# One tiled stretch for all K=64 tails of four row tiles, with a second xy tile in PSUM and the spectral pieces in the z banks

**Chip, cores, metric.** One core of one Trainium2 chip. Metric: device time of one execution in microseconds (us), lower is better.

## The reference

Forward and gradients of a gated sum of two branches over x (2048 x 576): a spectral filter (2-D real FFT, multiplication by a 2048 x 289 complex weight, inverse FFT) and a gated FFN of width 4608. Cut to what matters:

```python
def _A_ref(x, w_r, w_i):                      # spectral branch
    X = rfft2(x) * (w_r + 1j * w_i)
    return irfft2(X, s=(S, D))                # S, D = 2048, 576
def _B_ref(x, w_gate, w_up, w_down):          # FFN branch, F = 4608
    return (gelu(x @ w_gate) * (x @ w_up)) @ w_down
def _fwd(...):
    g = sigmoid((x * gate_w).sum(-1, keepdims=True))
    return g * _A_ref(...) + (1 - g) * _B_ref(...)
out, vjp = jax.vjp(_fwd, ...);  return out, *vjp(grad_out)
```

## The kernel before

A head transposes x and the output gradient and does the forward spectral pieces of x. Then come eighteen groups of 256 columns of F. In each group eight steps treat two row tiles (of 128 rows) each: `z` (output gradient times w_down), `xy` (x times w_gate and w_up), elementwise work on ScalarE and VectorE, and between them weight-gradient units (`wps`) of the group before and "pieces" of the spectral branch (`pf`). The last part (`acc`) reads the stored products back and is not touched. The contraction over 576 is 4 x 128 + 64; the 64-row tails of two row tiles sit in the two halves of the array (row tiling; the profile's form `64*128`). A run of such matmuls between full ones is called a tiled stretch here.

Some terms. Two steps, four row tiles, are a *pair*; a group has four. Groups are numbered from 0 and pairs from 1 through the kernel, so that pairs 1, 5, ... are the *first pairs* of groups. A piece is *evacuated* when ScalarE or VectorE has read it out of PSUM; only then can its banks be written again. The waits name a piece by what it is evacuated to: `Y` and `Vt` (forward pieces), `Xx`, `Xg` and `Vt` (middle ones), `ZT` (the first half of an inverse piece, `z(i)` in the code), `ev` and then `yo` (its second half, `d(i)`, called a d piece below). `z` in the profile is the FFN's tile alone.

The parts that matter, cut (`...`):

```python
ph = ...tile_pool(name="ph", bufs=1, space=PSUM)   # xy: 2 banks
pz = ...tile_pool(name="pz", bufs=1, space=PSUM)   # z: 2 banks
pw = ...tile_pool(name="pw", bufs=2, space=PSUM)   # weight gradients: 2 x 1 bank
pf = ...tile_pool(name="pf", bufs=1, space=PSUM)   # spectral pieces: 2 banks

def H_mm(g, tp):
    if tp % 2 == 0:
        zt[0] = pz.tile(...)
        ...  # 16 full matmuls (K=128), then the 4 tails (K=64, two at a time)
    xy = ph.tile([P, 2, 2 * FG], F32, tag="xy", name="xy")
    for tt, r in enumerate((LO, HI)):                     # row-tiled tails
        nc.tensor.matmul(xy[:, tt, :], lhsT=xT[r, 4, t0 + tt, :], rhs=wgu[r, 4, :], start=True, stop=False)
    ...  # 8 full matmuls

def d(i):   # inverse spectral piece: 4 full matmuls, 2 row-tiled
    def f():
        yps = pftile()
        ...
        nc.scalar.activation(ev[:], yps[:, 0, :DF], ACT.Copy, scale=scale)
        V.scalar_tensor_tensor(yo[:, 0:DF], yps[:, 1, :DF], scale, ev[:], op0=ALU.mult, op1=ALU.add)
        V.scalar_tensor_tensor(yo[:, D - 1:DF - 1:-1], yps[:, 1, 1:DF - 1], -scale, ev[:, 1:DF - 1], ...)
        LD.dma_start(dv[:, i, :], yo[:])
```

## Time and profile before

| | before |
|---|---|
| time, median of 3 (range) | 1528.66 us (1527.97 to 1532.15) |
| TensorE busy | 1462.9 us, 96% |
| first z matmul / first acc matmul | 61.4 / 1085.2 us |
| a group with middle spectral pieces / inverse ones / none | 54 / 56.6 to 58.6 / 48.8 us |

The group lengths are distances between the first z matmuls of groups in the trace. The lines are in the prediction. TensorE sets the time; what it loses must be sought in distances between the starts of its matmuls, as the ends are modelled. This is the stage of the inverse spectral pieces, from the windows view (window, its length, then busy us and instructions of TensorE, weight loads, VectorE, ScalarE, GpSimd, then TensorE's clock, share of the DMA engines, GB/s):

```profile
613.30:1009.10 395.80, 385.66 (x3086) 262.32 (x3136) 273.45 (x755) 249.76 (x501) 0.00 (x0) 1.00 0.44 121
```

TensorE is idle for 10 of 396 us there, at full clock.

### The profile page before, as it was taken

Reading aid. Unit: us, or ns where it says so; the run is one execution under the profiler, and the core shown is the slowest. Engines: PE = TensorE matmul, PEld = TensorE weight load, DVE = VectorE, ACT = ScalarE, POOL = GpSimd, SP = SyncE. Lnnn points to the kernel's source line nnn. Section 1 sums busy time; section 2 is a strip of 40 time slices with the busy share of each in tenths; the row PEclk is TensorE's granted clock in tenths of the full one; section 3 lists DMA queues with packets and bytes.
Section 4 is the critical chain, followed back from the end, with each engine's and each line's share of the span. In section 5 each row is a group of like instructions: output and inputs, shape, how many; then the busy total and the mean of one; then the engine's idle time right before and its main releaser. Section 6 shows DMA issues by size and latency. Waiting matters only on the chain.

```text
span 1530.2 us, 30042 instructions
## 1 busy us (share of the span) xinstructions
PE 1462.9 (96%) x11700; PEld 1052.8 (69%) x11824; DVE 845.8 (55%) x2237; ACT 699.4 (46%) x1361; POOL 21.8 (1%) x51
## 2 busy tenths in 40 slices
PE   7879998999999999999999999999998999999998
PEld 5535666666766766666666666677876777777776
DVE  6576666888888877666676666775023221211101
ACT  5565665676766766666666666664000000000000
POOL 1000000000000000000000000000000000000000
PEclk9899999999999999999999999999999999999999
DMA  5143234445445434434434434556999987878773
GB/s 182 43 113 102 84 109 125 119 132 147 135 141 146 129 115 138 119 100 120 126 99 135 135 107 123 147 131 136 265 212 213 189 164 155 173 154 170 150 154 65
DMA packets 503399, 210.49 MB, mean 138 GB/s; under 512 B 307606, under 2 KB 497112, under 8 KB 503256
## 3 DMA queue, kind: packets, MB, share of 16 engines
q1 hardware_dynamic: 499816, 202.83, 54.6%
q0 software_dynamic: 1632, 4.72, 1.2%
q8 instruction: 92, 1.51, 0.4%
q10 hardware_dynamic: 1808, 1.02, 0.2%
q14 instruction: 51, 0.42, 0.1%
HBM read 40.89 MB, written 93.82 MB: 88 GB/s over the span
## 4 chain that ended last, share of the span: by engine, by line
PE 66%; issue 24%; ACT 4%; DVE 3%; POOL 1%; SPq 1%; DMA 1%; POOLq 0%; DVEq 0%; ACTq 0%
PE wps L409 16%; PE xy L326 15%; PE z L315 8%; PE wps L392 8%; PE acc L851 3%; PE xy L323 2%; PE wps L420 2%; PE acc L893 2%; PE z L319 1%; PE pf L629 1%; PE fx L449 1%; PE pf L449 1%; PE pf L645 1%; ACT q L338 1%; ACT xb L339 1%
## 5 line engine op out<-in xcount | busy, mean ns | idle before, releaser
L326 PE MATMUL xy<-wgu,xT 128*128 128x512 bf16 x1028 | 256.1, 380 | 13.8 <-issue 10.8
L893 PEld LDWEIGHTS <-pin 128*128 128x128 bf16 x2304 | 225.4, 98 | 56.8
L409 PEld LDWEIGHTS <-xn 128*128 128x128 bf16 x2304 | 224.2, 98 | 36.7 <-issue 0.2
L326 PEld LDWEIGHTS <-xT 128*128 128x128 bf16 x1152 | 101.1, 98 | 142.7 <-issue 41.1
L337 ACT ACTIVATE da<-z,omg 128x256 bf16<-128x256 f32 x288 | 121.0, 473 | 108.6 <-PE z L319 108.6
L338 ACT ACTIVATE q<-xy 128x512 bf16<-128x512 f32 x144 | 86.0, 597 | 148.0 <-PE xy L326 147.9
L851 PE MATMUL acc<-wd_all,pin 128*128 128x288 bf16 x1152 | 145.4, 288 | 7.8 <-DMA pin<-scr 4.0
L392 PE MATMUL wps<-dB,A 128*128 128x288 bf16 x1152 | 150.0, 286 | 0.0
L315 PE MATMUL z<-wdT,dOT 128*128 128x256 bf16 x1152 | 142.4, 278 | 3.5 <-DVE Vt L471 3.5
L341 DVE TENSOR_SCALAR s<-q 128x512 bf16<-128x512 bf16 x144 | 42.0, 292 | 185.3 <-ACT q L338 185.2
L893 PE MATMUL acc<-wgT,pin 128*128 128x288 bf16 x1152 | 143.4, 286 | 0.0
L893 PE MATMUL acc<-wuT,pin 128*128 128x288 bf16 x1152 | 143.4, 286 | 0.0
L851 PEld LDWEIGHTS <-pin 128*128 128x128 bf16 x1152 | 113.3, 98 | 38.5 <-issue 4.7
L392 PEld LDWEIGHTS <-A 128*128 128x128 bf16 x1152 | 111.3, 98 | 32.9
L409 PE MATMUL wps<-dHg,xn 128*128 128x256 bf16 x1152 | 131.7, 273 | 0.0
L409 PE MATMUL wps<-dHu,xn 128*128 128x256 bf16 x1152 | 131.4, 273 | 0.0
L315 PEld LDWEIGHTS <-dOT 128*128 128x128 bf16 x1152 | 113.4, 100 | 22.1 <-issue 3.8
L903 ACT COPY f32t<-acc 128x576 f32<-128x576 f32 x16 | 10.2, 639 | 249.1 <-PE acc L893 249.1
L905 DVE SCALAR_TENSOR_TENSOR f32t<-gwf,dlog,f32t 128x576 f32<-128x576 f32 x16 | 13.1, 819 | 188.0 <-ACT f32t L903 188.0
L349 ACT ACTIVATE om<-s 128x512 bf16<-128x512 bf16 x144 | 92.4, 642 | 15.4 <-DVE s L342 14.7
L350 ACT ACTIVATE s<-s 128x512 bf16<-128x512 bf16 x144 | 90.7, 630 | 4.6
L340 ACT CAST hu<-xy 128x512 bf16<-128x512 f32 x144 | 86.9, 603 | 0.0
(183 smaller groups left out, 1729.9 us busy)
## 6 DMA issues: line engine op xcount, KB each, us to landing
scr<-A SPq DMA_DIRECT2D x144, 128.0 KB, 1.8
scr<-dHg SPq DMA_DIRECT2D x144, 128.0 KB, 1.9
scr<-dHu SPq DMA_DIRECT2D x144, 128.0 KB, 1.9
out_dram<-dw SPq DMA_DIRECT2D x67, 128.0 KB, 1.9
wd_all<-in_B_w_down_dram SPq DMA_DIRECT2D x3, 1728.0 KB, 15.3
out_dram<-dwd SPq DMA_DIRECT2D x34, 144.0 KB, 1.9
scr_p<-Vt SPq DMA_DIRECT2D x32, 144.5 KB, 2.2
Vp<-scr_p SPq DMA_DIRECT2D x16, 289.0 KB, 3.1
```

What stands on the lines that cost most here:

```text
L315: nc.tensor.matmul(zt[0][:, t % 2, (t - t0) // 2, :], lhsT=dOT[:, ci, t, :], rhs=wdT[:, ci, :], start=(t < t0 + 2 and ci == 0), stop=False)
L326: nc.tensor.matmul(xy[:, tt, :], lhsT=xT[:, ci, t0 + tt, :], rhs=wgu[:, ci, :], start=False, stop=(ci == 3))
L337: nc.scalar.activation(da[:, tt, :], da_ps[:, tt, :], ACT.Copy, scale=omg32[:, t0 + tt:t0 + tt + 1])
L338: nc.scalar.activation(q[:], hg, ACT.Square)
L340: nc.scalar.copy(hu[:], hu_ps)
L341: V.tensor_scalar(s[:], q[:], A_GELU, 1.0, op0=ALU.mult, op1=ALU.add)
L349: nc.scalar.activation(om[:], s[:], ACT.Sigmoid, scale=-2.0 * C_GELU)
L350: nc.scalar.activation(s[:], s[:], ACT.Sigmoid, scale=2.0 * C_GELU)
L392: nc.tensor.matmul(wps[:, :288], lhsT=tl(0, t)[:, fch * P:(fch + 1) * P], rhs=dB[:, t, h * 288:(h + 1) * 288], start=(t == 0), stop=(t == ...
L409: nc.tensor.matmul(wps[:, cc, :], lhsT=xn[:, t, (c0 + cc) * P:(c0 + cc + 1) * P], rhs=tl(k, t), start=(t == 0), stop=(t == T - 1))
L851: nc.tensor.matmul(bps[:, h, :288], lhsT=At[:, r, :], rhs=wd_all[:, fc, h * 288:(h + 1) * 288], start=(fc == 0), stop=(fc == NFC - 1))
L893: nc.tensor.matmul(xps[:, h, :288], lhsT=src[:, r, :], rhs=wT[:, h * 288:(h + 1) * 288], start=(k == 1 and f0 + r == 0), stop=(k == 2 and ...
```

## The change

Intent: fewer changes of TensorE's tiling mode. Four row tiles are taken together; all K=64 tails of z and of both xy tiles stand in one row-tiled stretch. For that two xy tiles must be open at once, and the two banks come from `pf`: from the second group on, the spectral pieces use the z banks. Spectral pieces are never row-tiled, their tails padded to full matmuls. Core of the diff:

```diff
-    ph = ps1.enter_context(tc.tile_pool(name="ph", bufs=1, space=PSUM))
+    ph = ps1.enter_context(tc.tile_pool(name="ph", bufs=2, space=PSUM))
-    pf = ps1.enter_context(tc.tile_pool(name="pf", bufs=1, space=PSUM))
+    pg = pgs.enter_context(tc.tile_pool(name="pg", bufs=1, space=PSUM))   # group 0 alone; then pw
 ...
     def H_mm(g, m):                          # m: one of four pairs of steps
+        for t in ts: ...                     # z, 16 full
+        for t in ts: ...                     # z, 4 tails
+        xy = [ph.tile([P, 2, 2 * FG], F32, tag="xy", name="xy") for _ in range(2)]
+        for t in ts: ...                     # xy, 4 tails
+        def full(k): ...                     # 8 full matmuls of tile k
 ...
     def pftile():
-        return pf.tile([P, 2, 512], F32, tag="pf", name="pf")
+        fctr[0] += 1
+        if pw is None and fctr[0] % 2:
+            return pg.tile([P, 2, 512], F32, tag="pg", name="pf")
+        return pz.tile([P, 2, 512], F32, tag="z", name="pf")
 ...             # a d piece: 6 full matmuls in place of 4 full and 2 tiled
-                    for lc in range(2): ...
-                for c, r in enumerate((LO, HI)):
-                    nc.tensor.matmul(yps[:, c, :DF], lhsT=Z[r, 4, :], rhs=tb.At2[r, :], start=False, stop=True)
+                    for lc in range(3): ...
 ...             # the loop over a group's pairs
+            z, xy_full = H_mm(g, m)
+            xy = xy_full(0)
+            das = H_da(m, z)
+            ta = H_ew1(xy)
+            for h in carry: h()               # first pair: last weight gradient of the group before
+            xy = xy_full(1)
+            k = 1 if n and hs else 0
+            if k or g == 0: fft_next()        # first piece
+            tc_ = H_ew1(xy)
+            H_ew2(g, 2 * m, ta, das[0])       # first tile: sigmoids, eight VectorE operations
+            def mid(): ... H_ew2(g, 2 * m + 1, tc_, das[1]) ...
+            if hs: hs[0]()                    # half a weight-gradient unit
+            run_W(hs[1:], n - k, mid)         # the other halves, with pieces 2 and 3 among them
```

More of the change, by code (lines that the diff above doesn't have):

```diff
@@ L40 @@
 LO, HI = slice(0, 64), slice(64, 128)
-L2 = DF - 64
+L2 = DF - P
 L2NEW = 256 - L2
@@ L66, in iotas @@
     G.iota(tb.dcol[:, 0:4], pattern=[[128, 4]], base=0, channel_multiplier=1, **kw)
-    for r in (LO, HI):
-        G.iota(tb.dcol[r, 4:5], pattern=[[0, 1]], base=512, channel_multiplier=1, **kw)
+    G.iota(tb.dcol[:, 4:5], pattern=[[0, 1]], base=512, channel_multiplier=1, **kw)
     tb.krow = res.tile([P, P], F32, name="krow")
@@ L112, in build_D, with sines @@
         V.scalar_tensor_tensor(y[:], X[:], -1.0, X[:], op0=ALU.mult, op1=ALU.max)
-        def sines(o=o, X=X, y=y):
-            nc.scalar.activation(o[:, :, 0, :], y[:], ACT.Sin, bias=tb.halfpi[:], scale=-step)
-            nc.scalar.activation(o[:, :, 1, :], X[:], ACT.Sin, scale=-step * EPS_SCALE)
+        r = LO if c0 == 4 else slice(0, P)
+        if c0 == 4:
+            nc.gpsimd.memset(o[HI, :, :, :], 0.0)
+        def sines(o=o, X=X, y=y, r=r):
+            nc.scalar.activation(o[r, :, 0, :], y[r], ACT.Sin, bias=tb.halfpi[r], scale=-step)
+            nc.scalar.activation(o[r, :, 1, :], X[r], ACT.Sin, scale=-step * EPS_SCALE)
         tb.late.append(sines)
@@ L253 @@
     ps1 = ExitStack()
-    ph = ps1.enter_context(tc.tile_pool(name="ph", bufs=1, space=PSUM))
+    ph = ps1.enter_context(tc.tile_pool(name="ph", bufs=2, space=PSUM))
     pz = ps1.enter_context(tc.tile_pool(name="pz", bufs=1, space=PSUM))
-    pw = ps1.enter_context(tc.tile_pool(name="pw", bufs=2, space=PSUM))
-    pf = ps1.enter_context(tc.tile_pool(name="pf", bufs=1, space=PSUM))
+    pgs = ExitStack()
+    pg = pgs.enter_context(tc.tile_pool(name="pg", bufs=1, space=PSUM))
+    pw = None
     g_bf = res.tile([P, T], BF16, name="g_bf")
@@ L264 @@
     tb.Rt = []
-    tb.At2 = res.tile([P, DF], BF16, name="At2")
+    tb.At2 = hres.tile([P, 2, DF], BF16, name="At2")
     hctr = [0]
@@ L270, in headps @@
         hctr[0] += 1
-        pool, tag = ((pf, "pf"), (ph, "xy"), (pz, "z"))[hctr[0] % 3]
+        pool, tag = ((pg, "pg"), (ph, "xy"), (pz, "z"), (ph, "xy"))[hctr[0] % 4]
         return pool, tag
@@ L292, in gate @@
     def gate():
-        lps = pw.tile([P, 512], F32, tag="wps", name="lps")
+        lps = head_tile()[:, 0]
         for t in range(T):
@@ L304, with H_mm @@
     kept = {}
-    zt = [None]
-    def H_mm(g, tp):
+    def H_mm(g, m):
         wgu, wdT = wts[g]
-        t0 = tp * TPB
-        if tp % 2 == 0:
-            zt[0] = pz.tile([P, 2, 2, FG], F32, tag="z", name="z")
-            for t in range(t0, t0 + 4):
-                for ci in range(4):
-                    nc.tensor.matmul(zt[0][:, t % 2, (t - t0) // 2, :], lhsT=dOT[:, ci, t, :], rhs=wdT[:, ci, :],
-                                     start=(t < t0 + 2 and ci == 0), stop=False)
-            for t in range(t0, t0 + 4):
-                r = (LO, HI)[t % 2]
-                nc.tensor.matmul(zt[0][:, t % 2, (t - t0) // 2, :], lhsT=dOT[r, 4, t, :], rhs=wdT[r, 4, :],
-                                 start=False, stop=t >= t0 + 2)
-        xy = ph.tile([P, 2, 2 * FG], F32, tag="xy", name="xy")
-        for tt, r in enumerate((LO, HI)):
-            nc.tensor.matmul(xy[:, tt, :], lhsT=xT[r, 4, t0 + tt, :], rhs=wgu[r, 4, :], start=True, stop=False)
-        for tt in range(TPB):
-            for ci in range(4):
-                nc.tensor.matmul(xy[:, tt, :], lhsT=xT[:, ci, t0 + tt, :], rhs=wgu[:, ci, :], start=False, stop=(ci == 3))
-        return xy[:, :, 0:FG], xy[:, :, FG:2 * FG], zt[0][:, :, tp % 2, :]
@@ L329, in H_ew1, with zo @@
-    def H_ew1(g, tp, pts):
-        hg, hu_ps, da_ps = pts
-        def ewt(tag):
-            return ew.tile([P, TPB, FG], BF16, tag=tag, name=tag)
-        xb, q, s, om, hu, da = (ewt(n) for n in ("xb", "q", "s", "om", "hu", "da"))
-        t0 = tp * TPB
-        for tt in range(TPB):
-            nc.scalar.activation(da[:, tt, :], da_ps[:, tt, :], ACT.Copy, scale=omg32[:, t0 + tt:t0 + tt + 1])
+        ts = range(4 * m, 4 * m + 4)
+        z = pz.tile([P, 2, 2, FG], F32, tag="z", name="z")
+        def zo(t):
+            return z[:, t % 2, t % 4 // 2, :]
@@ new lines, in H_mm @@
+        for t in ts:
+            for ci in range(4):
+                nc.tensor.matmul(zo(t), lhsT=dOT[:, ci, t, :], rhs=wdT[:, ci, :], start=(t % 4 < 2 and ci == 0), stop=False)
+        for t in ts:
+            r = (LO, HI)[t % 2]
+            nc.tensor.matmul(zo(t), lhsT=dOT[r, 4, t, :], rhs=wdT[r, 4, :], start=False, stop=t % 4 >= 2)
+        xy = [ph.tile([P, 2, 2 * FG], F32, tag="xy", name="xy") for _ in range(2)]
+        for t in ts:
+            r = (LO, HI)[t % 2]
+            nc.tensor.matmul(xy[t % 4 // 2][:, t % 2, :], lhsT=xT[r, 4, t, :], rhs=wgu[r, 4, :], start=True, stop=False)
@@ new lines, in full, with ewt, H_da @@
+        def full(k):
+            for t in ts[2 * k:2 * k + 2]:
+                for ci in range(4):
+                    nc.tensor.matmul(xy[k][:, t % 2, :], lhsT=xT[:, ci, t, :], rhs=wgu[:, ci, :], start=False, stop=(ci == 3))
+            return xy[k]
+        return z, full
+    def ewt(tag):
+        return ew.tile([P, TPB, FG], BF16, tag=tag, name=tag, bufs=3 if tag in ("da", "xb") else 2)
+    def H_da(m, z):
+        das = []
+        for k in range(2):
+            da = ewt("da")
+            for tt in range(TPB):
+                t = 4 * m + 2 * k + tt
+                nc.scalar.activation(da[:, tt, :], z[:, tt, k, :], ACT.Copy, scale=omg32[:, t:t + 1])
+            das.append(da)
+        return das
@@ L338, in H_ew1 @@
+    def H_ew1(xy):
+        xb, q, s, hu = (ewt(n) for n in ("xb", "q", "s", "hu"))
+        hg = xy[:, :, 0:FG]
         nc.scalar.activation(q[:], hg, ACT.Square)
         nc.scalar.copy(xb[:], hg)
-        nc.scalar.copy(hu[:], hu_ps)
+        nc.scalar.copy(hu[:], xy[:, :, FG:2 * FG])
         V.tensor_scalar(s[:], q[:], A_GELU, 1.0, op0=ALU.mult, op1=ALU.add)
@@ L344, in H_ew1, with H_ew2 @@
         V.tensor_tensor(q[:], xb[:], q[:], op=ALU.mult)
-        return xb, q, s, om, hu, da
-    def H_sig(tiles):
-        xb, q, s, om, hu, da = tiles
+        return xb, q, s, hu
+    def H_ew2(g, tp, tiles, da):
+        xb, q, s, hu = tiles
+        om = ewt("om")
         nc.scalar.activation(om[:], s[:], ACT.Sigmoid, scale=-2.0 * C_GELU)
         nc.scalar.activation(s[:], s[:], ACT.Sigmoid, scale=2.0 * C_GELU)
-    def H_ew2(g, tp, tiles):
-        xb, q, s, om, hu, da = tiles
         A = keepA.tile([P, TPB, FG], BF16, tag="A", name="A")
@@ L385, in tl, with halves, wtile, f @@
             return kt[t // TPB][k][:, t % TPB, :]
-        dwd_tiles = {}
+        dwd_tiles, wp = {}, {}
+        def halves(f):
+            return [lambda: f(0), lambda: f(1)]
+        def wtile(key):
+            if key not in wp:
+                wp[key] = pw.tile([P, TPB, FG], F32, tag="wps", name="wps")
+            return wp[key]
         def u_dwd(fch, h):
-            def f():
-                wps = pw.tile([P, 512], F32, tag="wps", name="wps")
-                for t in range(T):
+            def f(half):
+                wps = wtile(("d", fch, h)).rearrange("p a b -> p (a b)")
+                for t in range(8 * half, 8 * half + 8):
                     nc.tensor.matmul(wps[:, :288], lhsT=tl(0, t)[:, fch * P:(fch + 1) * P],
                                      rhs=dB[:, t, h * 288:(h + 1) * 288], start=(t == 0), stop=(t == T - 1))
+                if half == 0:
+                    return
                 if h == 0:
@@ L400, in f @@
                     wst[0].dma_start(out_6[r0:r0 + P, :], dwd[:])
-            return f
+            return halves(f)
         def u_dw(k, ov, c0):
-            def f():
-                late = k == 2 and c0 + TPB >= 4
-                wps = pw.tile([P, TPB, FG], F32, tag="wps", name="wps")
-                for cc in range(TPB):
-                    for t in range(T):
-                        nc.tensor.matmul(wps[:, cc, :], lhsT=xn[:, t, (c0 + cc) * P:(c0 + cc + 1) * P],
-                                         rhs=tl(k, t), start=(t == 0), stop=(t == T - 1))
+            def f(cc):
+                wps = wtile(("w", k, c0))
+                for t in range(T):
+                    nc.tensor.matmul(wps[:, cc, :], lhsT=xn[:, t, (c0 + cc) * P:(c0 + cc + 1) * P],
+                                     rhs=tl(k, t), start=(t == 0), stop=(t == T - 1))
+                if cc == 0:
+                    return
@@ L411, in f @@
                 dw = stage.tile([P, TPB, FG], BF16, tag="dw", name="dw")
-                (nc.scalar.copy if late else wevac)(dw[:], wps[:])
+                wevac(dw[:], wps[:])
                 wst[0].dma_start(ov[:, c0:c0 + TPB, fsl], dw[:])
-            return f
-        def u_tail():
-            wps = pw.tile([P, TPB, FG], F32, tag="wps", name="wps")
-            for t in range(T):
-                for k, r0 in ((1, 0), (2, 64)):
-                    nc.tensor.matmul(wps[r0:r0 + 64, 0, :], lhsT=xn[:, t, 512:576], rhs=tl(k, t),
+            return halves(f)
@@ L421, in u_tail, with tail @@
+        def tail(half):
+            wps = wtile("t")
+            for t in range(8 * half, 8 * half + 8):
+                for k, r in ((1, LO), (2, HI)):
+                    nc.tensor.matmul(wps[r, 0, :], lhsT=xn[:, t, 512:576], rhs=tl(k, t),
                                      start=(t == 0), stop=(t == T - 1))
+            if half == 0:
+                return
             dw = stage.tile([P, FG], BF16, tag="dwt", name="dwt")
             wevac(dw[:], wps[:, 0, :])
-            wst[0].dma_start(out_4[512:576, fsl], dw[0:64, :])
@@ L425, in u_tail @@
-            wst[0].dma_start(out_5[512:576, fsl], dw[64:128, :])
-        dw1, dw2 = ([u_dw(k, ov, c0) for c0 in range(0, 4, TPB)] for k, ov in ((1, o4v), (2, o5v)))
-        ud = [u_dwd(fch, h) for fch in range(FCH) for h in range(2)]
+            wst[0].dma_start(out_4[512:576, fsl], dw[LO, :])
+            wst[0].dma_start(out_5[512:576, fsl], dw[HI, :])
+        w = [u_dw(k, ov, c0) for k, ov in ((1, o4v), (2, o5v)) for c0 in range(0, 4, TPB)]
+        d = [u_dwd(fch, h) for fch in range(FCH) for h in range(2)]
@@ L428, in W_units @@
         if g == 0:
-            return dw1 + ud + [u_tail] + dw2
-        return [ud[0], dw1[0], ud[1], ud[2], ud[3], dw1[1], u_tail] + dw2
+            return [[w[0], halves(tail)], [w[1], d[0]], [d[1], d[2], d[3]], [w[2], w[3]], []]
+        return [[d[0]], [d[1], w[0]], [d[2], d[3], halves(tail)], [w[1], w[2]], w[3]]
     side = []
@@ L436, in gap @@
         pass
+    fctr = [0]
     def pftile():
-        return pf.tile([P, 2, 512], F32, tag="pf", name="pf")
+        fctr[0] += 1
+        if pw is None and fctr[0] % 2:
+            return pg.tile([P, 2, 512], F32, tag="pg", name="pf")
+        return pz.tile([P, 2, 512], F32, tag="z", name="pf")
     def fwd_units(src, dst, scale, ps=pftile, vevac=None):
@@ L447, in f @@
                 for c in range(2):
-                    for ci in range(4):
+                    for ci in range(5):
                         nc.tensor.matmul(yps[:, c, :DF], lhsT=src[:, ci, t, :], rhs=tb.Dt[ci][:, c, :],
-                                         start=(ci == 0), stop=False)
-                for c, r in enumerate((LO, HI)):
-                    nc.tensor.matmul(yps[:, c, :DF], lhsT=src[r, 4, t, :], rhs=tb.Dt[4][r, c, :], start=False, stop=True)
+                                         start=(ci == 0), stop=(ci == 4))
                 ys[t] = unit([2, DF], name="Y")
@@ L480, in tail_table @@
         nc.gpsimd.memset(tb.At2[:], 0.0)
-        for c in range(2):
-            LD.dma_start(tb.At2[64 * c + L2NEW:64 * c + 64, :], tb.Dt[2][0:DF - 256, c, :])
+        LD.dma_start(tb.At2[L2NEW:P, :, :], tb.Dt[2][0:DF - 256, :, :])
     def zipped(u1, u2):
@@ L625, in f @@
                 zf = zps[:].rearrange("p a b -> p (a b)")
-                for lc in range(2):
+                for lc, l0 in enumerate((0, P, L2)):
                     o = zf[:, lc * 256:(lc + 1) * 256]
                     for v in range(2):
-                        nc.tensor.matmul(o, lhsT=Vp[:, ii, v, lc * P:(lc + 1) * P],
+                        nc.tensor.matmul(o, lhsT=Vp[:, ii, v, l0:l0 + P],
                                          rhs=tb.B[:, 1 - v:3 - v, :].rearrange("q v m -> q (v m)"), start=(v == 0), stop=(v == 1))
-                for v in range(2):
-                    for c, r in enumerate((LO, HI)):
-                        nc.tensor.matmul(zf[r, 512:640], lhsT=Vp[:, ii, v, L2:DF], rhs=tb.B[:, 1 - v + c, :],
-                                         start=(v == 0), stop=(v == 1))
-                zt[i] = unit([5, P], name="ZT")
-                nc.scalar.copy(zt[i][:].rearrange("p a m -> p (a m)"), zf[:, 0:640])
+                zt[i] = unit([6, P], name="ZT")
+                nc.scalar.copy(zt[i][:].rearrange("p a m -> p (a m)"), zf[:, 0:768])
             return f
@@ L643, in f @@
                 for c in range(2):
-                    for lc in range(2):
-                        nc.tensor.matmul(yps[:, c, :DF], lhsT=Z[:, 2 * lc + c, :], rhs=tb.Dt[lc][:, c, :],
-                                         start=(lc == 0), stop=False)
-                for c, r in enumerate((LO, HI)):
-                    nc.tensor.matmul(yps[:, c, :DF], lhsT=Z[r, 4, :], rhs=tb.At2[r, :], start=False, stop=True)
+                    for lc in range(3):
+                        nc.tensor.matmul(yps[:, c, :DF], lhsT=Z[:, 2 * lc + c, :],
+                                         rhs=tb.Dt[lc][:, c, :] if lc < 2 else tb.At2[:, c, :],
+                                         start=(lc == 0), stop=(lc == 2))
                 ev = unit([DF], F32, name="ev")
@@ L707, with want @@
     n_slots = sum(1 for u in fft if not getattr(u, "noslot", False))
-    LAST = NG * NT - 16
-    PACE = [0, 1, 3, 4, 6, 7, 8, 10, 11]
-    slot0 = 2 * NT - 1
+    NPR = NT // 2
+    LASTP = NG * NPR - 7
     done = [0]
-    def want(step, half):
-        h = 2 * step + half
-        if h <= 2 * NT:
-            n = max(0, h - 1)
-        else:
-            tp = step % NT
-            n = slot0 + (n_slots - slot0) * ((step - tp - NT) / NT + (PACE[tp] + half * (PACE[tp + 1] - PACE[tp]) / 2) / PACE[NT]) \
-                / ((LAST - NT) / NT)
+    def want(pr):
+        n0 = 4 * NPR
+        n = 4 * (pr + 1) if pr < NPR else n0 + (n_slots - n0) * (pr + 1 - NPR) / (LASTP - NPR)
         return int(min(n, n_slots) + 1e-9)
-    def fft_until(n):
-        while done[0] < n:
-            fft_next()
-            done[0] += 1
     wgT_all = []
@@ L736, in load_wgT @@
             wgT_all.extend([u[:, 0], u[:, 1]])
+    wgT_from = 54
     def early_loads():
@@ L740, in early_loads, with run_W @@
         LD.dma_start(gwb[:], gate_w.partition_broadcast(P))
-    early = {1: early_loads}
-    wgT_from = 108
-    pend = []
-    carry = []
-    quota = [0, 1, 1, 1, 2, 1, 1, 1]
-    for g in range(NG):
-        for tp in range(NT):
-            step = g * NT + tp
-            fft_until(want(step, 0))
-            pts = H_mm(g, tp)
-            tiles = H_ew1(g, tp, pts)
-            fft_until(want(step, 1))
-            H_sig(tiles)
-            if carry:
-                carry.pop()()
-            H_ew2(g, tp, tiles)
-            if step in early:
-                early[step]()
-            if 6 <= step < 6 + T // 4:
-                for t in range(4 * (step - 6), 4 * (step - 6) + 4):
-                    V.tensor_scalar(dB[:, t, :], dB[:, t, :], omg32[:, t:t + 1], None, op0=ALU.mult)
-            if done[0] == n_slots or (step >= wgT_from and step % 4 == 0 and len(wgT_all) < 20):
+    def run_W(hs, n, mid=None):
+        total = max(len(hs), 1)
+        k = 0
+        for j in range(total):
+            while k < n and k * total <= j * n:
+                fft_next()
+                k += 1
+            if mid and 2 * j >= total - 1:
+                mid()
+                mid = None
+            if j < len(hs):
+                hs[j]()
+        while k < n:
+            fft_next()
+            k += 1
@@ new lines, with scale_dB, side_work, mid @@
+    carry, pend = [], None
+    scaled = [0]
+    def scale_dB(n):
+        for t in range(scaled[0], min(scaled[0] + n, T)):
+            V.tensor_scalar(dB[:, t, :], dB[:, t, :], omg32[:, t:t + 1], None, op0=ALU.mult)
+            scaled[0] = t + 1
+    for g in range(NG):
+        if g == 1:
+            pgs.close()
+            pw = ps1.enter_context(tc.tile_pool(name="pw", bufs=2, space=PSUM, **kw))
+        for m in range(NPR):
+            pr = g * NPR + m
+            n = want(pr) - done[0]
+            done[0] += n
+            hs = [h for u in pend[m] for h in u] if pend else []
+            def side_work():
+                for _ in range(3):
+                    if side:
+                        side.pop(0)()
+            if g == 0:
+                fft_next()
+            z, xy_full = H_mm(g, m)
+            xy = xy_full(0)
+            das = H_da(m, z)
+            ta = H_ew1(xy)
+            if g == 0:
+                fft_next()
+            for h in carry:
+                h()
+            carry = []
+            xy = xy_full(1)
+            k = 1 if n and hs else 0
+            if k or g == 0:
+                fft_next()
+            tc_ = H_ew1(xy)
+            H_ew2(g, 2 * m, ta, das[0])
+            def mid():
+                side_work()
+                H_ew2(g, 2 * m + 1, tc_, das[1])
+                side_work()
+            if hs:
+                hs[0]()
+            if g == 0:
+                fft_next()
+                mid()
+            else:
+                run_W(hs[1:], n - k, mid)
+            if pr == 1:
+                early_loads()
+            if (g, m) in ((0, 3), (1, 0)):
+                scale_dB(T // 2)
+            if done[0] == n_slots or (pr >= wgT_from and pr % 2 == 0 and len(wgT_all) < 20):
@@ L764 @@
                 load_wgT()
-            if tp == 1 and g >= 1 and g + 1 < NG:
+                if done[0] == n_slots:
+                    load_wgT()
+            if m == 0 and g >= 1 and g + 1 < NG:
                 wts[g + 1] = load_w(g + 1)
-            for _ in range(quota[tp]):
-                if pend:
-                    pend.pop(0)()
-            for _ in range(3):
-                if side:
-                    side.pop(0)()
-        assert len(pend) <= 1
-        carry = pend
+        carry = pend[4] if pend else []
@@ L808 @@
     wst[0] = nc.scalar
-    for u in carry + pend:
-        u()
+    for h in carry + [h for us in pend[:4] for u in us for h in u] + pend[4]:
+        h()
     ps1.close()
```

## The prediction

> **What bounds the kernel now.** I read the page first (busy shares, slices), then the windows by stage, then the list of waits, then the timeline of single pairs of row tiles, where one program step is a tile of two rows and a pair (four row tiles) is the new unit of work.
>
> ```profile
> PE 1462.9 (96%) x11700; PEld 1052.8 (69%) x11824; DVE 845.8 (55%) x2237; ACT 699.4 (46%) x1361; POOL 21.8 (1%) x51
> ...
> PE   7879998999999999999999999999998999999998
> ...
> DVE  6576666888888877666676666775023221211101
> ...
> ```
>
> ```profile
> L326 PE MATMUL xy<-wgu,xT 128*128 128x512 bf16 x1028 | 256.1, 380 | 13.8 <-issue 10.8
> ```
>
> TensorE bounds it: only the first tenth shows it below nine tenths. The head ends at 61.4 us, where the first z matmul starts. Eighteen weight groups of four pairs follow until 1085.2 us, then the part with "acc", which the change leaves alone (445 us). From the starts of the z matmuls a group takes 57.1, 57.7, 54.8, 57.5, 57.1, 53.9, 54.4, 53.9 us and so on, and 48.8 us for the last full one, which has no spectral pieces. What that group must cost at the trace's own spacing of starts (109 ns at 256 columns, 122.5 at 288, 216 at 512; the two halves of a K=64 or 64-column pair together) is: z 7.9, xy 15.5, weight gradients 7.8 + 14.0 + tail 1.7, in all 47.0 us. The missing 1.8 us is nine stretches of tiled matmuls at 0.2 us. So the FFN groups have no stall to win, only that 0.2 us:
>
> ```profile
> 601.14 1.91 PE L315 MATMUL z<-wdT,dOT 128*128 128x256 bf16 x16
> 602.98 0.39 PE L319 MATMUL z<-wdT,dOT 64*128 64x256 bf16 x4
> ...
> 607.72 0.39 PE L323 MATMUL xy<-wgu,xT 64*128 64x512 bf16 x2
> 608.04 1.90 PE L326 MATMUL xy<-wgu,xT 128*128 128x512 bf16 x7
> ```
>
> Sixteen starts of 109 ns would end at 602.88; the tiled one starts at 602.98, so going in costs 0.1 us. The tiled xy pair at 607.72 is worth 216 ns, and the next full matmul starts 320 ns later: 0.1 us for going out.
>
> The exception is group 0: no weight gradients yet, TensorE is busy 40.6 of the 55 us from 60 to 115, and it waits for ScalarE and VectorE through a single xy tile and a single spectral tile.
>
> The line that matters for what the change may cost:
>
> ```profile
> 786.73 0.30 PE L648 MATMUL pf<-At,ZT 64*128 64x289 bf16 x2
> 786.96 1.92 PE L315 MATMUL z<-wdT,dOT 128*128 128x256 bf16 x16
> ...
> 788.35 0.42 DVE L364 TENSOR_TENSOR dHu<-da,xb 128x512 bf16<-128x512 bf16 x1
> 788.68 0.68 DVE L376 CAST dw<-wps 128x512 bf16<-128x512 f32 x1
> ...
> 789.29 0.45 DVE L652 SCALAR_TENSOR_TENSOR yo<-pf,ev 128x289 bf16<-128x289 f32 x1
> ...
> 789.65 0.45 DVE L653 SCALAR_TENSOR_TENSOR yo<-pf,ev 128x287 bf16<-128x287 f32 x1
> ```
>
> An inverse spectral piece ("d") ends near 787.0, but its tile "pf" is read to the end only at 790.1, because the reading stands in VectorE's queue behind the elementwise work of the step. It costs nothing here: pf has banks of its own, and z starts at once at 786.96.
>
> **What the Trainium skill says.** "TensorEngine Tiling (Array Packing)", Tiling Modes, Key Properties: changing the tiling mode drains TensorE. The trace agrees: 205 ns instead of 109 on the way in, about 320 instead of 216 on the way out. "TensorE: Matmul & The Clock Gate", Part 1: ScalarE and VectorE are strict FIFO queues. Agrees: the read of pf above waits for older work. The same part says that an idle array falls to half clock; the first sixteen z matmuls, after 3.49 us of idleness, take 3.57 us instead of 1.75. "PSUM — Partial Sum Buffer", Specifications (TRN2): eight banks of 512 FP32 values. Before, xy 2, z 2, weight gradients 2, pf 2 fill them; a second xy tile can only come from pf, so the spectral pieces move into z. No run shows a ninth bank, and the program's tiles add up to eight.
>
> **The change part by part.**
> (a) *One tiled stretch a pair.* Two stretches before (z with the first xy, then the second xy), one after: 72 fewer at 0.2 us, -14.4 us. The row-tiled weight-gradient tails stay in one piece in TensorE's order.
> (b) *Untiled spectral pieces.* Forward: 8 x 123 + one pair 123 + 0.2 us becomes 10 x 123: -0.08 us, 32 times. Inverse d: 4 x 123 + 123 + 200 = 815 becomes 6 x 123 = 738. Inverse z: 4 x 109 + 112 + 190 = 738 becomes 6 x 109 = 654. 32 each. Together -7.7 us; ScalarE copies 768 instead of 640 columns.
> (c) *Group 0.* With two xy tiles and two spectral tiles VectorE sets the pace: per pair 2 x (1.4 + 3.1) us elementwise and 2 x 0.75 of Vt, some 10.5 to 11 us against 14.3 now. Over four pairs with a slow first one, -9 us beyond (a). Head, four tiles in rotation for three: -1 us.
> (d) *The shared z banks.* Now a piece must be evacuated before the next piece, and before the next pair's z, can start. I lay a pair out by hand, 0 at the z tails, with durations start to start from the trace (da 0.42, q/xb/hu 0.48 each, the sigmoids 0.6 to 0.66 each, VectorE's eight operations after them 3.1, yo 0.9). TensorE: tails to 0.75, xy to 2.48 and 4.2, first piece to 4.7-4.9, half a dWd unit 0.98, second piece, more weight gradients, perhaps a third piece. The program order puts ScalarE: da, three copies (to 4.1), first evacuation (5.4 to 5.75), three copies of the second tile (7.2), two sigmoids (8.4), second evacuation. So the second piece, computed at about 6.6, is released at 8.7 if ScalarE reads it, and at 12.05 if it is a d: ev on ScalarE, then yo behind eight operations that run 8.0 to 11.1. TensorE comes to need the banks between 8.9 and 12.6, depending on the pair.
> First pair of a group: 3.5 us of carried weight gradient stand ahead of the second xy, which then ends at 7.7, and only d0 (2 x 0.98 us) stands behind. Two middle-stage pieces: released 12.2, needed 10.64, stall 1.55. Three: the third waits 1.55, and its own evacuation stands behind two more sigmoids: 3.1 in all. With inverse pieces 1.3 to 7.6.
> Sums from the piece order in TensorE's program: middle stage, first pairs only, 3 x 3.1 + 3 x 1.55 = 14 us. Inverse stage, 25 pairs: the seven first pairs 2.5 + 5.4 + 1.3 + 4.8 + 6.5 + 4.4 + 7.6 = 32; of the other eighteen, pieces (d,z) 1, (z,d) 3, (z,d,z) 10, (d,z,d) 13, together 27. Forward 1. In all 74 us, against some 5 us of stall there now.
>
> Net by this table: 1529 - 14 - 8 - 10 + 69 = 1566. I take a tenth off the stalls, as the table starts each pair with the slowest engine order and I may have an evacuation too late: 1560.
>
> **The rivals.**
> *R1, the stalls are small:* then the gains stand alone, 1529 - 32 = 1497 plus a few, about 1500. For it: queues drain whenever TensorE waits, ScalarE is only about two thirds busy here, and the design looks tuned (the carried unit between the two xy). Against it: the 3.1 us from a d to its last read is measured, already with less work queued ahead than the new order puts there.
> *R2, stalls also lower the clock:* stalls of 4 to 7 us in first pairs let the clock drop, as at 61.4 us, each adding up to 1.8 us: 1575 to 1595. Against it: a few events only.
> *R3, ScalarE or VectorE becomes the bound:* VectorE has 9 us a pair, 13 with products, of 13.5 to 14. Close, but before is no different: 1505 to 1530.
>
> **Range and chances.** The gains (22 us of matmul and drain, 10 us of group 0) are firm to some 5 us; the loss may be anything from 10 to 90. Hence 1508 to 1596. Beyond -2% is under 1498, which needs R1 almost pure: 0.13. Above 1559 is slower: the table says so by a little, R2 more: 0.49. The rest 0.38.
>
> **What would show it.** Right: start to start of the z matmuls 11.5 us in a group's first two pairs where no pieces are left; a last full group of 48.0 instead of 48.8; group 0 near 48; waits of z and pf matmuls for yo and for ScalarE's evacuations summing to 50 us or more, largest in first pairs and between the start of the inverse stage and the group where the pieces end; groups of 60 us and more there against 57 to 58.6. Wrong: waits of TensorE of a few us in all (then R1), or groups 5 to 8 at or below 53.1.

## The result

| | before | after |
|---|---|---|
| median of 4 (range) | 1529.57 (1527.97 to 1532.15) | 1579.21 (1575.12 to 1581.59) |
| ratio, 95% interval | | 1.032 (1.029 to 1.035) |
| span in the profile, mean clock | 1530.2, 0.992 | 1573.3, 0.981 |

Ratios here and below are the mean time of one kernel's fast runs over that of the other's fast runs of the same rounds, so not quite the ratio of the medians. The change makes the kernel 3.2% slower. All outputs are right. The prediction was 1560 us, within 1508 to 1596, with "slower" as the likeliest class.

The page after the change, busy shares and slices:

```profile
PE 1468.2 (93%) x11760; PEld 1074.2 (68%) x11760; DVE 844.5 (54%) x2243; ACT 685.5 (44%) x1355; POOL 22.3 (1%) x51
...
PE   7989999799999999989989888799998999999998
```

The work is nearly the same; TensorE's share fell by three points. Most of the new eights and one seven stand between 0.67 and 1.02 ms, where the inverse pieces run; the other new seven, in the eighth slice, is the single wait of 8 us at pair 17, told of below. The windows view of that stage, to be set beside the line of before:

```profile
607.60:1018.00 410.40, 360.35 (x2779) 250.86 (x2778) 249.03 (x689) 223.48 (x452) 0.00 (x0) 0.96 0.36 104
```

Now TensorE is idle for 50 of 410 us, and its clock has gone from 1.00 to 0.96. What it waited for, from the list of waits of TensorE in the groups (waiter, releaser: us in total, times, longest):

```profile
PE z L320 <- DVE yo L674: 21.7, 12, 4.9
PE pf L655 <- DVE yo L674: 17.7, 12, 4.1
PE z L320 <- ACT Vt L618: 12.3, 4, 8.0
PE z L320 <- ACT Y L484: 6.3, 5, 1.7
PE pf L667 <- DVE yo L674: 4.4, 2, 4.0
PE z L320 <- ACT ZT L658: 3.8, 4, 1.4
```

All six are waits of a z or pf matmul for the last reader of a spectral piece: with the smaller lines of the same kind 77 us, 44 of them for `yo`. A first pair of a group in the timeline (start us, us, engine, line, operation, [idle before <- releaser]):

```profile
941.82 0.41 PE L667 MATMUL pf<-Dt,ZT 128*128 128x289 bf16 x2
...
942.07 0.29 PE L667 MATMUL pf<-At,ZT 128*128 128x289 bf16 x1
...
942.19 1.15 PE L412 MATMUL wps<-dB,A 128*128 128x288 bf16 x8
...
942.73 0.66 ACT L364 ACTIVATE om<-s 128x512 bf16<-128x512 bf16 x1
...
943.42 0.63 ACT L365 ACTIVATE s<-s 128x512 bf16<-128x512 bf16 x1
943.42 0.43 DVE L369 TENSOR_TENSOR om<-om,q 128x512 bf16<-128x512 bf16 x1
...
943.96 0.40 ACT L672 ACTIVATE ev<-pf 128x289 f32<-128x289 f32 x1
...
946.14 0.42 DVE L376 TENSOR_TENSOR dHu<-da,xb 128x512 bf16<-128x512 bf16 x1
...
946.48 0.46 DVE L673 SCALAR_TENSOR_TENSOR yo<-pf,ev 128x289 bf16<-128x289 f32 x1
...
946.85 0.45 DVE L674 SCALAR_TENSOR_TENSOR yo<-pf,ev 128x287 bf16<-128x287 f32 x1
...
947.35 1.03 PE L320 MATMUL z<-wdT,dOT 128*128 128x256 bf16 x4 [4.02 <-DVE yo L674]
```

The d piece is computed by about 942.3. `ev` stands behind two sigmoids on ScalarE and starts at 943.96; `yo` stands behind eight operations on VectorE and ends at 947.3. In between TensorE has one half unit of weight gradient (1 us) and then nothing: z needs the banks that the piece still holds. In the kernel before a late reading cost z nothing, as z had its own banks; it delayed only some of the next pieces (y4_beforecopy below).

Where the 43 us between the two profiles come from: head -1.7 (first z at 59.7), group 0 -11.9 (45.2 us long), the other groups +60.1, the last part -3.4. The medians are 50 us apart: the profiled execution of before took 1531.99 us, near the top of its range, and that of after 1575.12 us, the lowest of its four.

### The profile page after: what moved, and what is told of

Its sections match the earlier page's. It is cut to its first block, busy times and chain, and to the rows that moved or that the text cites. A ratio compares the mean times of both kernels' runs of the same rounds, so it can differ in the third digit from the quotient of the medians.

```text
span 1573.3 us, 29838 instructions
## 1 busy us (share of the span) xinstructions
PE 1468.2 (93%) x11760; PEld 1074.2 (68%) x11760; DVE 844.5 (54%) x2243; ACT 685.5 (44%) x1355; POOL 22.3 (1%) x51
## 3 DMA queue, kind: packets, MB, share of 16 engines
q10 hardware_dynamic: 1808, 1.02, 0.2%
## 4 chain that ended last, share of the span: by engine, by line
PE 56%; issue 23%; DVE 9%; ACT 5%; POOL 1%; DMA 1%; SPq 1%; POOLq 0%; DVEq 0%; ACTq 0%
PE xy L332 16%; PE wps L429 13%; PE z L320 9%; PE wps L412 5%; PE acc L909 3%; PE xy L327 2%; PE acc L951 2%; PE wps L442 2%; PE z L323 1%; PE pf L655 1%; PE pf L478 1%; ACT q L352 1%; DVE om L374 1%; DVE A L372 1%; ACT xb L353 1%
## 5 line engine op out<-in xcount | busy, mean ns | idle before, releaser
L332 PE MATMUL xy<-wgu,xT 128*128 128x512 bf16 x1152 | 264.8, 380 | 0.0
L332 PEld LDWEIGHTS <-xT 128*128 128x128 bf16 x1152 | 106.9, 98 | 146.8 <-issue 32.1
L345 ACT ACTIVATE da<-z,omg 128x256 bf16<-128x256 f32 x288 | 113.3, 475 | 193.6 <-PE z L323 193.0
L320 PE MATMUL z<-wdT,dOT 128*128 128x256 bf16 x1152 | 150.3, 288 | 46.8 <-DVE yo L674 21.7
L320 PEld LDWEIGHTS <-dOT 128*128 128x128 bf16 x1152 | 116.7, 103 | 74.3 <-issue 31.5
L412 PE MATMUL wps<-dB,A 128*128 128x288 bf16 x1152 | 156.5, 286 | 0.0
L429 PE MATMUL wps<-dHg,xn 128*128 128x256 bf16 x1152 | 136.1, 274 | 0.0
L963 DVE SCALAR_TENSOR_TENSOR f32t<-gwf,dlog,f32t 128x576 f32<-128x576 f32 x16 | 13.1, 818 | 186.6 <-ACT f32t L961 186.6
```

Of the source, the lines that this page charges most:

```text
L320: nc.tensor.matmul(zo(t), lhsT=dOT[:, ci, t, :], rhs=wdT[:, ci, :], start=(t % 4 < 2 and ci == 0), stop=False)
L332: nc.tensor.matmul(xy[k][:, t % 2, :], lhsT=xT[:, ci, t, :], rhs=wgu[:, ci, :], start=False, stop=(ci == 3))
L345: nc.scalar.activation(da[:, tt, :], z[:, tt, k, :], ACT.Copy, scale=omg32[:, t:t + 1])
L412: nc.tensor.matmul(wps[:, :288], lhsT=tl(0, t)[:, fch * P:(fch + 1) * P], rhs=dB[:, t, h * 288:(h + 1) * 288], start=(t == 0), stop=(t == ...
L429: nc.tensor.matmul(wps[:, cc, :], lhsT=xn[:, t, (c0 + cc) * P:(c0 + cc + 1) * P], rhs=tl(k, t), start=(t == 0), stop=(t == T - 1))
```

## The experiments

Theory A: the time goes to waits for shared PSUM banks, held until a read comes up in its engine's queue. Theory B: the new order gives ScalarE or VectorE a worse schedule as such, whatever the banks. In the first four, all edits are to the changed kernel, save for x4_untiled.

**x1_copy: ScalarE copies a d piece out; VectorE reads SBUF.**

```diff
-                nc.scalar.activation(ev[:], yps[:, 0, :DF], ACT.Copy, scale=scale)
-                V.scalar_tensor_tensor(yo[:, 0:DF], yps[:, 1, :DF], scale, ev[:], ...)
+                nc.scalar.activation(ev[:], yps[:, :, :DF], ACT.Copy, scale=scale)   # ev: [2, DF]
+                V.scalar_tensor_tensor(yo[:, 0:DF], ev[:, 1, :], 1.0, ev[:, 0, :], ...)
```

> Theory A (shared z banks are held until the evacuation comes up in a queue; TensorE waited 77 us for that, 44 of them for yo on VectorE): here ScalarE copies both halves of a d piece to SBUF, so VectorE no longer reads PSUM there. The 44 us of waits for yo go, some 12 us of them come back as waits for ScalarE, the clock recovers a little: about 1545 us (1535 to 1555). Theory B (the time went to ScalarE or VectorE as a whole, which do more or worse ordered work): nothing is taken off either engine, ScalarE gets 0.24 us more per piece: 1579 us or slower.

Measured: 1531.38 us, ratio to before 0.9998 (0.9985 to 1.0012). 48 us came back, more than expected: all waits for `yo` are gone, and of those for ScalarE few were added:

```profile
PE z L320 <- ACT Vt L618: 12.3, 4, 8.0
...
PE z L320 <- ACT ZT L658: 5.5, 4, 1.5
PE z L320 <- ACT ev L672: 3.6, 3, 1.3
PE pf L655 <- ACT ev L672: 2.5, 2, 1.3
```

What stands in VectorE's queue ahead of its read was thus worth nearly the whole net loss of 50 us, though not all of the stalls: as the gains of the change count against them, the stalls are larger than the net loss, and x3_bank and y1_copybank get more back. All of the gain lies in groups 10 to 16, which have the inverse pieces.

**x2_early: the second piece's evacuation ahead of the first tile's chain; TensorE's order is the same.**

```diff
             tc_ = H_ew1(xy)
+            if hs:
+                hs[0]()
+                if g and n > k:
+                    fft_next()
             H_ew2(g, 2 * m, ta, das[0])
```

> TensorE's order is unchanged; only the evacuation of the second piece is issued ahead of the first tile's sigmoids and elementwise chain. Theory A: second pieces are released 1.3 us (ScalarE) to 3 us (VectorE) earlier, the waits fall from 77 to about 35 us, the third pieces keep theirs: about 1535 us (1525 to 1550). Theory B: same work on every engine, so 1575 to 1580 us.

Measured: 1568.13 us, 1.0242 (1.0228 to 1.0256). A miss: 11 us, not 45. The waits moved:

```profile
PE z L320 <- DVE yo L674: 27.4, 8, 6.6
...
PE pf L655 <- DVE yo L674: 2.4, 6, 0.5
PE pf L667 <- DVE yo L674: 1.3, 2, 1.0
```

Pieces hardly wait for the `yo` of the piece before any more (22 us in the changed kernel, 4 now), but ScalarE and VectorE now wait for the second piece first, both chains of elementwise work end later, and a d in last place is read later still: z waits 27 us for it, up to 6.6 at a time. I had held the third pieces' release fixed; in queues that are worked off in the program's order, as the timeline above shows them, it is not. This run does not tell A from B by its size; x3_bank does.

**x3_bank: pieces 2 and 3 of a pair use the xy tiles, which z does not need.**

```diff
+        pctr[0] += 1                      # set to 0 at each pair
+        if pw is not None and pctr[0] > 1:
+            return ph.tile([P, 2, 512], F32, tag="xy", name="pf")
         return pz.tile([P, 2, 512], F32, tag="z", name="pf")
```

> From the second group on, the first piece of a pair goes to the z banks, the second and third to the xy tiles, which z does not need and which the next pair needs 2 us later. Orders are unchanged. Theory A: waits fall to about 20 us, nearly all before the xy tails of pairs whose last piece is a d: about 1520 us (1510 to 1535). Theory B: 1575 to 1580 us.

Measured: 1516.67 us, 0.9902 (0.9887 to 0.9917), as A expected. In the two traces the order of work on TensorE, ScalarE and VectorE is the same, instruction by instruction but for missing records, so B can't explain 62 us. What is left stands ahead of the xy tails:

```profile
PE xy L327 <- DVE yo L678: 13.4, 8, 3.9
...
PE xy L327 <- ACT Vt L622: 7.3, 1, 7.3
PE z L320 <- ACT Y L488: 5.5, 4, 1.7
```

**x4_untiled: the kernel before with the untiled spectral pieces alone** (the hunks of the change for `L2`, `Dt`, `At2` and the forward, z and d pieces, nothing else).

> The kernel before with the untiled spectral pieces alone. If a tiled stretch costs 0.2 us of drain as the spacing of starts says, the 96 pieces save 0.08 us each, 7.7 us in all, less what the head hides: ratio 0.996 (1522 to 1526 us). If the drain were hidden by other waits, ratio 1.000; if the larger ScalarE copy or the extra matmul columns mattered, above 1.000.

Measured: 1524.48 us, 0.9961 (0.9948 to 0.9973): 6 us faster, of the 7.7 that the drain, the extra time around a tiled stretch, would give.

**y1_copybank: x1_copy and x3_bank together.**

> x1_copy and x3_bank together. Theory A: of the 1517 us of x3_bank the 13 us that the xy tails wait for yo go, and about half of what runs at half clock; the wait of 7 us for one Vt and those of group 0 stay: about 1502 us (1496 to 1508), ratio 0.981. Rival (the copy's gain of 48 us in x1_copy came from ScalarE and VectorE order, not from the banks): then it adds as much again here, well under 1490, or nothing, 1517.

Measured: 1498.92 us, 0.9798 (0.9785 to 0.9811), 18 us under x3_bank, as expected.

**y2_side: y1_copybank with the spectral products ahead of the second tile's chain.**

```diff
                 side_work()
-                H_ew2(g, 2 * m + 1, tc_, das[1])
                 side_work()
+                H_ew2(g, 2 * m + 1, tc_, das[1])
```

> y1_copybank with both portions of the spectral products issued before the second tile's elementwise chain instead of one before and one behind. If the one wait of 7 to 8 us for Vt (its SBUF buffer is freed by a product that stands behind that chain) is only a place in VectorE's queue, it shrinks by about 3 us: 3 us under y1_copybank. If the products now delay the chain and with it TensorE's next needs: the same or slower.

Measured: 1496.71 us, 0.9773 (0.976 to 0.9786). The wait for the one Vt fell from 7.3 to 4.3 us, and the time by some 3 us.

**y3_split: y1_copybank with the second tile's tails moved back.**

```diff
         def full(k):
+            if k:
+                tails(1)          # K=64 matmuls of xy tile 1; tails(0) stays in the first stretch
```

> y1_copybank with the second xy tile's K=64 tails moved back ahead of its own full matmuls: 72 more tiled stretches, all else equal. If each costs the 0.2 us of drain read from the spacing of starts: 14.4 us slower than y1_copybank, or 11 where a pair waits anyway (the second xy tile is needed later): 1513 to 1517 us. Rival (the drain is hidden behind waits or weight loads): within 3 us of y1_copybank.

Measured: 1506.65 us, 0.9841 (0.9827 to 0.9854): 7.7 us over y1_copybank, a miss: the least expected was 11. In the trace each added stretch shows the 0.1 us on either side: eight groups grow by 0.85 us each, as four stretches of 0.2 us would make them. But the second xy tile is now needed 2 us later. y1_copybank loses about 11.7 us between the tails of its first and second xy tile (spacing of starts beyond the usual 0.21 us, after group 0); y3_split, ahead of its second tile's tails, loses only the wait for the one Vt, some 5.6 us: 6 us that the split gives back.

**y4_beforecopy: the kernel before with the copy of x1_copy alone.**

> The kernel before with the copy of x1_copy alone. It was worth 48 us in the changed kernel. Theory A: here pf has its own banks and z never waits for yo, so it is worth 0 to 2 us (TensorE waits 1.7 us for yo in this trace, 3.4 in weight loads): ratio 0.998 to 1.001. Rival (the copy is simply better for VectorE or ScalarE): tens of us faster here too.

Measured: 1525.61 us, 0.9963 (0.9949 to 0.9976). A miss of some 4 us: 6 us, not 0 to 2. The six groups with inverse pieces are 341.7 us long in all against 347.0. So even with banks of its own the next piece sometimes waited for `yo`: by the spacing of starts, the z pieces of before came 5.4 us late in all, and those of y4_beforecopy do not. The list of waits had 1.7 us of it on TensorE and 3.4 on the weight loads, and I had taken only the first as lost, though the prediction itself counts some 5 us of stall there. The argument stands with that correction: the copy is worth 48 us where the banks are shared and 6 where they are not.

**z1_pace: y2_side with one or two pieces in first pairs and up to three in the others.**

```diff
-        n = ... n0 + (n_slots - n0) * (pr + 1 - NPR) / (LASTP - NPR)
+        q, r = divmod(pr + 1 - NPR, NPR)
+        pos = NPR * (q + (0.0, 0.12, 0.41, 0.70)[r])
+        n = ... n0 + (n_slots - n0) * pos / (LASTP - NPR)
```

> y2_side with the pieces dealt unevenly: one or two in a group's first pair, up to three in the others. In y1_copybank TensorE lost some 6 us in short waits for the xy banks ahead of the tails, besides the one for Vt, most where a first pair has its last piece right ahead of the next pair. If those are the evacuations' places in the queues, 4 to 6 us less than y2_side: ratio 0.973 to 0.975. Rival (the waits move to the pairs that get three pieces): as y2_side, 0.977.

Measured: 1489.18 us, 0.9716 (0.9696 to 0.9736), some 9 us better than y2_side by the ratios, more than the 4 to 6 expected; by the spacing of starts, the waits ahead of xy tails account for about 4 of them (8.7 us in y2_side, 4.5 here), and what gave the rest was not sought. This version beats both kernels: 2.8% under before, 5.7% under the change by medians. Its largest remaining waits:

```profile
PE z L320 <- ACT Y L488: 5.5, 4, 1.7
PE xy L327 <- ACT Vt L622: 3.9, 1, 3.9
...
```

**z3_pacesplit: z1_pace with the split of y3_split**, now with almost no waits to give back.

> z1_pace with the second tile's K=64 tails split off again, as y3_split. y3_split was only 7.7 us over y1_copybank; I put that down to 72 drains of 0.2 us, 14 us, less some 6 us of waits for the second xy tile that the later need avoids. If so, here, with those waits gone, the split costs 11 to 14 us. Rival (a stretch is worth only 0.1 us in the whole): 7 to 8 us again.

Measured: 1500.18 us, 0.9787 (0.9767 to 0.9808): 11.0 us over z1_pace. The 72 stretches are worth 14 us by their spacing; 11 arrive here, as some waits (2.5 of the 4.5 us ahead of the xy tails in z1_pace) still go. Fifteen of the eighteen groups grow by 0.6 to 0.85 us, and the one with the wait for Vt shrinks by 3.0. This upholds the reading of y3_split.

## Why the prediction was right, step by step

**(a) One tiled stretch, -14.4 us: right.** The last group, without pieces, runs in pairs of 11.5, 11.5 and 11.9 us; with the last pair of the group before it, 13.1 us and without pieces too, that makes 48.0 us as foretold (no single full group of the changed kernel is without pieces). The gain itself was tested by putting it back: 7.7 us among waits, 11.0 almost without; no run shows the whole 14.4 at once.

**(b) Untiled pieces, -7.7 us: right,** 6 us in x4_untiled.

**(c) Group 0, -9 us beyond (a): right,** 57.1 to 45.2 us is -11.9, of which some 0.8 is (a). That two xy and two spectral tiles are the cause rests on the trace alone; no run took them apart. The reason given, that VectorE sets the pace there, holds only in part: in a pair of 10.9 us VectorE is busy for 9.7 us, and TensorE, busy for about as long, runs through but for 1.4 us in which z waits for `Y`, a spectral piece that ScalarE reads behind two sigmoids. Head: -1.7 for -1.

**(d) The stalls: right in mechanism and close in size.** I compared my table with the spacing of starts ahead of z and pf matmuls beyond their nominal one, pair by pair. Inverse stage: first pairs of groups 33.2 us (the table's seven add up to 32.5), the others 25.9 (27). A recount that takes the drain as nominal gives 32.6 and 24.3. Singly: the first pairs 41, 45, 49, 53, 57, 61, 65 lost 2.7, 5.6, 1.5, 5.2, 6.5, 4.3 and 7.4 us, and the table had 2.5, 5.4, 1.3, 4.8, 6.5, 4.4 and 7.6. Middle stage: first pairs with two pieces 1.7 (1.55), with three 3.2 (3.1). A hand replay of three queues with the trace's own durations was good enough here, because in these traces each engine takes its work in the program's order.

**What was mis-sized or misread.** The first reading of the page was loose: besides the first tenth, slices 7, 31 and 40 of the kernel before are below nine tenths too; nothing rests on it. I took a tenth off the stalls (6 us), which was wrong: the table was right as it stood. Two terms were missing or too small. One is pair 17, the first of group 4, 9.9 us where the table had 3.1:

```profile
287.59 0.64 ACT L618 CAST Vt<-pf 128x578 bf16<-128x578 f32 x1 [6.52 <-DVE o L577]
...
288.28 3.42 PE L320 MATMUL z<-wdT,dOT 128*128 128x256 bf16 x16 [7.97 <-ACT Vt L618]
```

Vt's SBUF buffer is freed by a spectral product "o" that stands behind the second tile's chain on VectorE (in the program all such tiles rotate through one set of 19 buffers); with shared banks z waits behind Vt. y2_side, which moves the products forward, takes 3 us off it. In the kernel before, the same wait of Vt was 3.0 us and only a piece stood behind it. The other is the clock, below. By its own 1560, 2.0% over the kernel before, the table left the class "slower" near a toss-up (0.49); that it came out clearly owes to these two terms.

**The rivals.** R1 (stalls small) fell. R2 (clock) was true as an addition: the z matmuls above take 3.42 us, where sixteen take 1.91 otherwise, right after the wait of 8 us. Summed over the matmuls of the groups that run at half rate, the excess is 13.8 us after, 5.1 before, 3.2 in y1_copybank (a second count: 14.8, 6.1 and 3.2): about 9 us of the loss. With the 7 us of pair 17 that is a little more than the 13 us between the table's 1566 and the result's 1579. "TensorE: Matmul & The Clock Gate" in the Trainium skill, Part 1, says that idleness brings the array to half clock; the trace agrees. That the stalls lower the clock is shown by its return once they are gone, from 0.981 to 0.989 in x1_copy and 0.993 in y1_copybank. R3 (an engine becomes the bound) fell: x3_bank got 62 us back with the same work in the same order on TensorE, ScalarE and VectorE.

What stays open: how much of the clock's part could be had without removing the stalls; no run held one fixed.

## What to carry to other kernels

Before two users share a PSUM tile, work out when its last reader comes up in its engine's queue, not how long the reading takes: here 0.9 us of reading kept z waiting for 4 us. A saving on the bound engine (22 us of drains and padded matmuls) is real only if the buffer that pays for it is free in time. When a good idea turns out slower, look for the one wait that eats it: one copy on ScalarE, other banks for the second and third piece, the spectral products moved forward, and fewer pieces where little work hides them turned +3.2% into -2.8%.

## What the Trainium skill lacked or had wrong

- "TensorEngine Tiling (Array Packing)", Tiling Modes, Key Properties, says that a mode change drains TensorE and gives no size. Here: 205 ns from a full 256-column matmul to a tiled one instead of 109, and 308 to 320 ns from a tiled 512-column pair to a full one instead of 216, so 0.2 us a stretch; 72 stretches put back cost 7.7 and 11.0 us in two kernels.
- The same page counts PSUM pressure of tiling as banks and evacuation speed. What decided here is on no page in this form: how long a tile is held is set by the place of its last read in a queue, 5 us from the end of a d piece to the end of `yo` in the pair shown, for 0.9 us of VectorE work.
- "TensorE: Matmul & The Clock Gate", Part 1: that idleness brings half clock is confirmed; the runs add its price in a kernel that is busy 93% of the time: beside 77 us of waits, up to 8 us long, 13.8 us of half-rate excess, against 5.1 us before.
